# Order of the loads behind a first batch of attention, small copies on another engine, and a reduction held back

## The chip, the cores and the metric

One core of one Trainium2 chip. The metric is the device time of one execution in microseconds (us). Each kernel is executed several times; a number such as "842.15 median" is over its runs in the fast state, and all runs compared here are of that state. The profile is one execution, and its span is 1.7 to 1.9 us shorter than the time of the same execution.

Engines are named as in the profile: PE is TensorE (matmuls), DVE is VectorE, ACT is ScalarE, POOL is GpSimd, SP is the engine that issues the DMA transfers here.

## The reference

Four batches of block-sparse attention (8 heads, 768 positions, head dimension 64): each query sees the keys within 16 positions and, for each block of 32 keys, the maximum of the keys and the mean of the values. The result, 768 x 512 per batch, goes through a Fourier mix, a normalization and a two-layer MLP.

```python
k_sum = k.reshape(B, H, nb, block, D).max(axis=3)
v_sum = v.reshape(B, H, nb, block, D).mean(axis=3)
scores_l = scale * np.matmul(q, k.transpose(0, 1, 3, 2))      # masked to |i - j| < 16
scores_s = scale * np.einsum('bhsd,bhnd->bhsn', q, k_sum) + np.log(block)
# softmax over both, times [v, v_sum]; heads side by side -> x (B, 768, 512)
X = np.fft.fft(np.fft.fft(x, axis=1), axis=2)
u = x + np.real(X)
un = (u - mean(u)) / np.sqrt(var(u) + 1e-06)
out = u + np.maximum(un @ w_ch1, 0.0) @ w_ch2                 # 512 -> 2048 -> 512
```

## The kernel before

The change sits in the first 60 us. The first batch's attention goes by pairs of heads, g = 0 to 3. For each pair, `prepare` transposes keys and queries on PE, copies them out of PSUM on ACT (`kt`, `qt`) and takes the block maxima of the keys on DVE (`km`). `wide_scores` gives the probabilities `p`, and `wide_values` multiplies them by the values (`vw`, loaded by `load_values`, in rows of 256 bytes). The result x is "folded" on DVE (sums and differences of mirrored columns), and the folded tiles are the input of the first Fourier matmuls, `y`; then come the mix matmuls `mx`, the normalization, transposes `unt`, and the hidden layer `hx`. Beside this runs the second batch's attention. `load(b, g)` loads keys and queries of a pair, `load_raw(n)` loads packed weights ("words") up to the n-th, `block_sums` loads and adds the values of a block, `near` is a mask table.

```python
def first_attention():
    ...
    for g in range(NP - 1):
        p[g + 1] = wide_scores(0, g + 1, ...)
        wide_values(0, g, p[g], x)
        load_values(*following(0, g, 2))          # g = 1: the last pair's values
        for par in range(2):
            fold_sequence(par, g)
        if g == 0:
            get_tables(0)                         # fs, fs, fd
        if g < NP - 2:
            prepare(0, g + 2)
            load(1, g)                            # next batch's keys and queries
            sum_values(0, g + 1)
        if g == 0:
            load_raw(2)                           # weight words
            fetch(out=near, ...)
        ...
    fold_halves(0, 0)
    wide_values(0, NP - 1, p[NP - 1], x)
    for par in range(2):
        ...
        fold_ends(0, par, ...)
```

```python
# prepare(b, g), after the transposes
    for s in range(2):
        nc.scalar.copy(out=dst[...], in_=ps[D * s:D * (s + 1)])    # kt, then qt
nc.vector.tensor_reduce(out=km[:, 0:nb], in_=kt[...], op=ALU.max, axis=AX.X)

# fold_ends(b, par, zw, fg): three small copies among the DVE folds
nc.scalar.copy(out=fg[:, :, 0:DM:HD], in_=zw[:, :, 0:DM:HD])              # 128 x 6
tt(fg[:, :, 1:Q], ..., ADD)
nc.scalar.copy(out=zqs[b][:, par], in_=zw[:, :, Q])                       # 128 x 3
...
nc.scalar.copy(out=fg[:, :, DM - 1:DM], in_=zw[:, :, HD + Q:HD + Q + 1])  # 128 x 3

# the main part
with tc.manual_schedule(engines={PE, DVE}):       # order as written; elsewhere a scheduler orders
    first_attention()
load_raw(4)
...
block_sums(1, 0)
def second_attention():
    prepare(1, 0)
    ...
drive((gen_fourier(0), 4, 600), (first(weights, 66), 12, 0), (first(attn, 6), 1, 0))
```

## Time and profile before

| | before |
|---|---|
| time, median of 4 | 842.15 us (842.01 to 842.78) |
| span of the profiled run, mean clock | 839.8 us, 0.989 |
| PE busy | 808.4 us, 96% |
| longest PE wait | 8.8 us, for the last pair's values |
| first y, first mx, first unt, first hx | 59.26, 71.97, 88.68, 95.73 us |
| first o, first ox (second layer), end | 150.51, 237.06, 839.8 us |

The last two rows are landmarks: the start of the first matmul of each stage. Where the kernel runs the same matmuls afterwards, a change can be followed as the shift of each landmark, and the difference between two neighbouring shifts says in which stage time was won or lost.

How PE reaches the first Fourier matmul is seen in its timeline (start, us, engine, line, operation, output<-inputs, sizes, count):

```profile
58.55 0.77 PE L756 MATMUL sc<-qt,kt 64*64 64x32 f32 x36
59.26 2.56 PE L1070 MATMUL y<-fs,fold 128*128 128x193 f32 x8
```

Scores of the next batch (sc) stand ahead of y in PE's order and fill its time while the folds are made, so y follows them without a gap.

### The profile page before, as it was taken

Reading aid. Unit: us, or ns where it says so; the run is one execution under the profiler, and the core shown is the slowest. Engines: PE = TensorE matmul, PEld = TensorE weight load, DVE = VectorE, ACT = ScalarE, POOL = GpSimd, SP = SyncE. Lnnn points to the kernel's source line nnn. Section 1 sums busy time; section 2 is a strip of 40 time slices with the busy share of each in tenths; the row PEclk is TensorE's granted clock in tenths of the full one; section 3 lists DMA queues with packets and bytes.
Section 4 is the critical chain, followed back from the end, with each engine's and each line's share of the span. In section 5 each row is a group of like instructions: output and inputs, shape, how many; then the busy total and the mean of one; then the engine's idle time right before and its main releaser. Section 6 shows DMA issues by size and latency. Waiting matters only on the chain.

```text
span 839.8 us, 14695 instructions
## 1 busy us (share of the span) xinstructions
PE 808.4 (96%) x6074; PEld 578.8 (69%) x6074; DVE 487.7 (58%) x1117; ACT 255.2 (30%) x567; POOL 12.8 (2%) x21
## 2 busy tenths in 40 slices
PE   8959899999999999999999999999999999999997
PEld 5748655545578855786668875788667875786586
DVE  4758989986996743543357822552347842532352
ACT  3523847542635123113233404120322502101100
POOL 0000000000000200011000000000000000000000
PEclk9969999999999999999999999999999999999999
DMA  9995799959633276255552244413412225205001
GB/s 227 244 230 86 165 282 245 298 198 321 212 116 124 76 271 170 87 114 193 132 120 89 78 171 171 126 26 103 158 46 81 77 82 232 88 0 219 1 26 54
DMA packets 101612, 120.55 MB, mean 144 GB/s; under 512 B 50560, under 2 KB 83552, under 8 KB 101344
## 3 DMA queue, kind: packets, MB, share of 16 engines
q1 hardware_dynamic: 100848, 119.31, 48.7%
q8 instruction: 50, 0.82, 0.4%
q10 hardware_dynamic: 688, 0.20, 0.1%
q14 instruction: 26, 0.21, 0.1%
HBM read 96.96 MB, written 22.54 MB: 142 GB/s over the span
## 4 chain that ended last, share of the span: by engine, by line
PE 83%; DVE 6%; DMA 4%; ACT 4%; SPq 1%; issue 1%; ACTq 0%; DVEq 0%
PE hx L1171 18%; PE ox L1235 17%; PE hz L1171 9%; PE oz L1235 9%; PE y L1070 4%; PE hy L1171 4%; PE oy L1235 4%; PE o L1212 3%; PE mx L1027 2%; PE sc L756 2%; DMA vb<-in_v_dram 2%; ACT qt L696 1%; ACT kt L696 1%; PE y L1074 1%; PE unt L1149 1%; PE av L789 1%
## 5 line engine op out<-in xcount | busy, mean ns | idle before, releaser
L1171 PE MATMUL hx<-u,w 128*128 128x384 f32 x512 | 187.2, 492 | 6.9 <-DVE h L562 2.8
L1171 PEld LDWEIGHTS hx<-u,w 128*128 128x128 f32 x512 | 94.5, 190 | 72.2 <-DVE h L562 6.4
L1171 PE MATMUL hz<-u,w 128*128 128x384 f32 x256 | 93.5, 487 | 0.1
L1235 PE MATMUL ox<-w,s 128*128 128x256 f32 x336 | 81.5, 381 | 0.3
L1235 PE MATMUL oz<-w,s 128*128 128x256 f32 x336 | 80.7, 379 | 0.0
L1235 PE MATMUL ox<-w,h 128*128 128x256 f32 x336 | 78.4, 381 | 0.0
L1171 PEld LDWEIGHTS hz<-u,w 128*128 128x128 f32 x256 | 48.4, 190 | 34.5 <-ACT h L1188 1.3
L562 DVE TENSOR_TENSOR x<-ox,x 128x256 f32<-128x256 f32 x84 | 35.4, 422 | 62.1 <-PE ox L1235 62.0
L1235 PEld LDWEIGHTS ox<-w,h 128*128 128x128 f32 x336 | 63.3, 190 | 10.7 <-DVE x L562 1.1
L1235 PEld LDWEIGHTS oz<-w,s 128*128 128x128 f32 x336 | 63.5, 190 | 8.3
L1235 PEld LDWEIGHTS ox<-w,s 128*128 128x128 f32 x336 | 62.5, 190 | 9.2 <-DVE x L562 1.1
L562 DVE TENSOR_TENSOR h<-hx,h 128x384 f32<-128x384 f32 x32 | 17.8, 555 | 65.8 <-PE hx L1171 65.8
L1181 ACT COPY h<-hx 128x384 f32<-128x384 f32 x32 | 15.3, 477 | 129.1 <-PE hx L1171 117.4
L562 DVE TENSOR_TENSOR h<-hy,h 128x384 f32<-128x384 f32 x32 | 17.8, 556 | 59.2 <-PE hy L1171 56.0
L1171 PE MATMUL hy<-u,w 128*128 128x384 f32 x128 | 48.2, 499 | 0.0
L1212 PE MATMUL o<-w,h 128*128 128x512 f32 x96 | 42.8, 597 | 0.0
L1235 PE MATMUL oy<-w,h 128*128 128x256 f32 x168 | 39.9, 379 | 0.0
L1197 ACT ACTIVATE h<-hx 128x384 f32<-128x384 f32 x32 | 15.6, 488 | 79.4 <-PE hx L1171 79.4
L1070 PE MATMUL y<-fs,fold 128*128 128x193 f32 x192 | 37.5, 342 | 0.2
L1171 PEld LDWEIGHTS hy<-u,w 128*128 128x128 f32 x128 | 24.7, 194 | 17.6 <-DVE w L562 0.8
L1070 PEld LDWEIGHTS y<-fs,fold 128*128 128x128 f32 x192 | 31.7, 193 | 6.3 <-issue 4.9
L1235 PEld LDWEIGHTS oy<-w,h 128*128 128x128 f32 x168 | 31.9, 190 | 4.3
(138 smaller groups left out, 1075.6 us busy)
## 6 DMA issues: line engine op xcount, KB each, us to landing
w<-dw SPq DMA_DIRECT2D x44, 896.0 KB, 5.6
words<-in_moe_w_ch_dram SPq DMA_DIRECT2D x32, 512.0 KB, 6.7
dw<-w SPq DMA_DIRECT2D x12, 896.0 KB, 7.0
vw<-in_v_dram SPq DMA_DIRECT2D x47, 192.0 KB, 5.7
kn<-in_k_dram SPq DMA_DIRECT2D x16, 384.0 KB, 4.5
qn<-in_q_dram SPq DMA_DIRECT2D x16, 384.0 KB, 5.4
out_dram<-x SPq DMA_DIRECT2D x24, 256.0 KB, 2.0
fs<-c_fs SPq DMA_DIRECT2D x8, 579.0 KB, 3.5
```

The source lines that it names most:

```text
L562: nc.vector.tensor_tensor(out=out, in0=in0, in1=in1, op=op)
L696: nc.scalar.copy(out=dst[D * e:D * (e + 1), s:S:2], in_=ps[D * s:D * (s + 1)])
L756: nc.tensor.matmul(ps[h][r:r + 64, i, :], kt[rows, o:o + 64], qt[rows, o:o + BLOCK], start=True, stop=True)
L789: nc.tensor.matmul(av[r][32 * j:32 * (j + 1), t, :], p[rows, h, i - NB2 * h, :], vw[rows, i, :], start=(t == 0), stop=False, skip_group_ch ...
L1027: nc.tensor.matmul(out, y[:, g], table, start=True, stop=last, skip_group_check=True)
L1070: nc.tensor.matmul(y, fgs[par][:, st, P * g:P * (g + 1)], fs[par][:, g % 2, st, :], start=(st == 0), stop=(st == HT - 1))
L1074: nc.tensor.matmul(ps[0:1, par:par + F2 + 1], zq[:, par, s2:s2 + 1], fs[par][:, 0, s2, :], start=False, stop=False, skip_group_check=True)
L1171: nc.tensor.matmul(ps, w[:, a, kk, :], u[:, r, kk, :], start=start and kk == 0, stop=stop and kk == 1, skip_group_check=True)
L1181: nc.scalar.copy(out=c11, in_=X)
L1197: nc.scalar.activation(out=c21, in_=X, func=AF.Relu)
L1212: nc.tensor.matmul(ps, h[:, n, hf, P * t:P * (t + 1)], wt[2, b, j][:, 2 * hf:2 * hf + 2, :], start=(n, hf) == (0, 0), stop=(n, hf) == (NC ...
L1235: nc.tensor.matmul(ps, left[a][:, n, :], wt[2, b, j][:, r, :], start=start and n == 0, stop=stop and n == NC - 1, skip_group_check=True)
```

## The change

Its intent: the last pair's values are needed at 41.6 us, but next batch's keys and queries, weight words and `near` are issued ahead of them. The change puts them behind. It takes six small copies off ACT, and ties the next batch's key maxima on DVE behind the folds, so that a late `kt` cannot hold the folds.

```diff
@@ prepare
-        nc.vector.tensor_reduce(out=km[:, 0:nb], in_=kt[...], op=ALU.max, axis=AX.X)
+        with tc.issue_after(marks["fold", 0]) if (b, g) == (1, 0) else ExitStack():
+            nc.vector.tensor_reduce(out=km[:, 0:nb], in_=kt[...], op=ALU.max, axis=AX.X)
@@ first_attention
                 prepare(0, g + 2)
-                load(1, g)
                 sum_values(0, g + 1)
-            if g == 0:
+            if g == NP - 3:
+                load_raw(1)
+                load(1, 0)
                 load_raw(2)
-                fetch(out=near, in_=dr["near"].ap()...)
-            if g == NP - 3:
                 sum_values(0, g + 2)
@@ fold_ends
-        nc.scalar.copy(...)                       # three of them
+        copy = nc.scalar.copy if b else nc.gpsimd.tensor_copy
+        copy(...)                                 # three of them
@@ main part
         first_attention()
+    fetch(out=near, in_=dr["near"].ap()...)
     load_raw(4)
+    load(1, 1)
```

The numbers of most later lines rise by one to four: L740 is L741 in the changed kernel, L1070 is L1072, L1171 is L1173.

More of the change, by code (lines that the diff above doesn't have):

```diff
@@ L696, in prepare @@
                         nc.scalar.copy(out=dst[D * e:D * (e + 1), s:S:2], in_=ps[D * s:D * (s + 1)])
-        nc.vector.tensor_reduce(out=km[:, 0:nb], in_=kt[:, W:W + S].rearrange("p (n f) -> p n f", f=BLOCK),
-                                op=ALU.max, axis=AX.X)
+        with tc.issue_after(marks["fold", 0]) if (b, g) == (1, 0) else ExitStack():
+            nc.vector.tensor_reduce(out=km[:, 0:nb], in_=kt[:, W:W + S].rearrange("p (n f) -> p n f", f=BLOCK),
+                                    op=ALU.max, axis=AX.X)
         nat[b, g] = qt
@@ L828, in first_attention @@
                 prepare(0, g + 2)
-                load(1, g)
                 sum_values(0, g + 1)
-            if g == 0:
+            if g == NP - 3:
+                load_raw(1)
+                load(1, 0)
                 load_raw(2)
-                fetch(out=near, in_=dr["near"].ap().rearrange("p (h i) c -> p h i c", h=2))
-            if g == NP - 3:
                 sum_values(0, g + 2)
@@ L863, in fold_ends @@
             zqs[b] = spool.tile([P, 2, HT], FP, tag="zq", bufs=2, name=f"zq_{b}")
-        nc.scalar.copy(out=fg[:, :, 0:DM:HD], in_=zw[:, :, 0:DM:HD])
+        copy = nc.scalar.copy if b else nc.gpsimd.tensor_copy
+        copy(out=fg[:, :, 0:DM:HD], in_=zw[:, :, 0:DM:HD])
         tt(fg[:, :, 1:Q], zw[:, :, 1:Q], zw[:, :, HD - 1:Q:-1], ADD)
-        nc.scalar.copy(out=zqs[b][:, par], in_=zw[:, :, Q])
+        copy(out=zqs[b][:, par], in_=zw[:, :, Q])
         nc.vector.memset(fg[:, :, Q:Q + 1], 0.0)
         tt(fg[:, :, Q + 1:HD], zw[:, :, 1:Q], zw[:, :, HD - 1:Q:-1], SUB)
-        nc.scalar.copy(out=fg[:, :, DM - 1:DM], in_=zw[:, :, HD + Q:HD + Q + 1])
+        copy(out=fg[:, :, DM - 1:DM], in_=zw[:, :, HD + Q:HD + Q + 1])
         tt(fg[:, :, HD + 1:HD + Q], zw[:, :, HD + 1:HD + Q], zw[:, :, DM - 1:HD + Q:-1], SUB)
@@ L1321, in _main_program @@
         first_attention()
+    fetch(out=near, in_=dr["near"].ap().rearrange("p (h i) c -> p h i c", h=2))
     load_raw(4)
+    load(1, 1)
     nc.vector.memset(vs, 0.0)
```

## The prediction

> **What bounds the kernel now.** I read the page first. TensorE (PE) is busy 96% of an 839.8 us span and holds 83% of the chain that ended last, so nearly all of the kernel is matmul time that this change does not touch. What can move is idle PE time, so I read PE's waits next, longest first:
>
> ```profile
> PE av L740 <- DMA vw<-in_v_dram: 8.8, 1, 8.8
> PE hx L1171 <- DVE h L562: 2.8, 2, 1.5
> PE hx L1171 <- ACT h L1181: 2.4, 3, 1.1
> PE sc L717 <- DVE km L697: 1.8, 2, 1.2
> ```
>
> Columns: total us, times, longest. One wait stands out: the value matmuls of the first batch's last pair of heads wait once, 8.8 us, for their values (vw) to come from memory. Everything else is under 3 us. The chain in order of time shows where that wait comes from (start, us, what):
>
> ```profile
> 39.95 1.64 PE av L740 x48
> 41.60 1.60 SPq L549
> 43.25 7.01 DMA vw<-in_v_dram
> 50.26 0.14 issue
> 50.40 3.07 PE av L740 x47
> 53.47 0.85 PE qk L694 x3
> ```
>
> Pair 2's values product runs at 39.95 and takes 1.64 us; pair 3's would follow at 41.6 and starts at 50.40. It then takes 3.07 us for the same 48 matmuls, so there is a second cost besides the wait. The timeline of the DMA-issuing engine says why the values are late:
>
> ```profile
> 33.42 0.38 SPq L549 DMA_DIRECT2D kn<-in_k_dram  x1
> 33.90 0.62 SPq L549 DMA_DIRECT2D qn<-in_q_dram  x1
> 34.61 4.92 SPq L549 DMA_DIRECT2D words<-in_moe_w_ch_dram  x2
> 39.58 1.28 SPq L549 DMA_DIRECT2D near<-c_near  x1
> 40.96 7.61 SPq L549 DMA_DIRECT2D vw<-in_v_dram  x6
> ```
>
> Next batch's keys and queries, two pieces of weight words and the table near are issued ahead of vw, though none is needed before 53 us. The table by stretches shows the two costs together (us; then busy time of PE, PEld, DVE, ACT, POOL; granted clock, DMA share, GB/s):
>
> ```profile
> 34.00:38.00 4.00, 3.10 (x40) 2.08 (x38) 3.92 (x5) 2.46 (x5) 0.00 (x0) 1.00 0.98 356
> 38.00:42.00 4.00, 3.55 (x74) 2.72 (x74) 2.73 (x7) 1.16 (x3) 0.14 (x1) 1.00 1.10 326
> 42.00:46.00 4.00, 0.00 (x0) 0.00 (x0) 2.98 (x7) 0.20 (x1) 0.00 (x0) 1.00 1.16 307
> 46.00:50.00 4.00, 0.00 (x0) 0.00 (x0) 0.00 (x0) 0.00 (x0) 0.00 (x0) 0.50 0.89 107
> 50.00:56.00 6.00, 5.60 (x60) 5.20 (x60) 1.97 (x5) 1.55 (x4) 0.14 (x1) 0.50 1.22 224
> 60.00:64.00 4.00, 4.00 (x15) 2.44 (x15) 4.00 (x11) 0.95 (x4) 0.00 (x0) 0.61 1.08 271
> ```
>
> PE does nothing from 41.6 to 50.4 while the DMA engines are full, and the clock falls to half at 46, because PE was idle, and again from about 59.7 to 63.1.
>
> **What the Trainium skill says.** "TensorE: Matmul & The Clock Gate", part 1 (the HAM clock gate): the clock is halved after an idle window and restored after a busy one, windows of 3413 ns that run freely. The trace agrees: in half-microsecond slices the clock changes at about 46.0, 56.3, 59.7 and 63.1, which are multiples of 3.41 us apart. "DMA: Bandwidth & Descriptors", section Queues, rings and completion order: each DMA engine consumes one issuer's descriptors in ring order. The trace agrees in the order of landing (issue plus time to landing: kn 41.4, qn 42.8, words 44.3 and about 46.3, near 48.3, vw 49.3 to 50.9). Same page, Why small descriptors are slow: 256-byte descriptors lose bandwidth; here the vw rows (256 bytes) move at about 130 to 160 GB/s against 326 to 356 GB/s for the longer ones. "GPSIMD Engine Reference", section 4.1: one-input elementwise work there is roughly at line rate. In the trace two 128x24 copies on GpSimd take 0.37 us together, and ScalarE takes 0.19 to 0.20 us for each of the small fold copies, so the move should cost nothing.
>
> **The change part by part.**
>
> Values earlier. The order of instructions in the built kernel puts the six vw transfers directly behind the Fourier tables (fs, fs, fd), so issue can start at 33.4 in place of 40.96. They need pair 1's product to be done, which it is at 31.3. In front of them in the ring no longer stand kn, qn (384 KB each), two words (512 KB each) and near (384 KB): 2176 KB, 2.23 MB. At 326 to 356 GB/s that is 6.3 to 6.8 us, so vw lands at 50.3 - 6.5 = about 43.7. A check from the other side: fd lands at 39.6, vw is 560 KB at 0.15 MB/us, 3.8 us, giving 43.4. The values product then runs from 43.8 to 45.5, at full clock (1.67 us, as for pair 2). The wait becomes about 2.2 us, not zero.
>
> Keys and queries later. Before, kn had landed at 41.4 and cost nothing. Now kn, qn and the first words go behind vw. The issuing queue itself blocks when much is outstanding (one 20 KB vw issue took 3.92 us), so I put the first words' issue at about 41.5, kn at 42.5 and qn at 43. With 3.4 and 4.4 us to landing, as those two took at 48.7 and 49.1 with little ahead of them, plus 1 to 1.5 us for the words ahead, kn lands at about 47 and qn at 48.5. This is a new wait of PE, 1.5 us after the values product. From the first key transposes to the first score matmul the chain before takes 57.52 - 53.40 = 4.1 us: transposes, four kt copies (2.04 us) and two of the four qt copies (1.0 us) on ScalarE. At full clock some 0.3 us less. In the new PE order one score matmul stands before the Fourier matmuls y, so y starts at about 47 + 3.9 = 50.9 in place of 59.26: 8.4 us earlier.
>
> Key maxima behind the folds. In the trace before, the reduction km (0.95 us) sits in VectorE's order ahead of the folds and waits 1.1 us for kt. Behind the folds it lets them start when x is ready: values end 45.5, four x pieces and the subtraction 2.0 us, two folds 1.0, first end fold 0.5, so y's input is there at about 49.2, before kt and qt. With the reduction in its old place the folds would end at about 52 and hold y by 1 us. So this part is worth about 1 us, already contained in the 50.9.
>
> Small copies. Six ScalarE copies of 0.19 us go, 1.1 us off an engine with a 30% share. They free y from waiting behind the kt and qt copies in ScalarE's order. GpSimd has nothing else to do. Worth 0 to 0.5 us, also contained.
>
> What is given back. Before y, the kernel before had already done 40 score matmuls and two ss products (0.30 + 0.83 + 0.77 = 1.9 us in the timeline); now all but one come after the mix matmuls, so 1.6 to 1.8 us of PE work goes behind. And the clock: between 45.5 and 50.9 PE has only some 1 us of work, so a 3.41 us window will nearly surely be idle enough and y begins at half clock until a full window has passed, costing half of 3.4 to 6.8 us less what passed before; I take 2.5 us. The kernel before loses half of 3.4 us, 1.7, there. Extra loss 0.8.
>
> Sum: 8.4 - 1.7 - 0.8 = 5.9 us. After that PE is dense, but between 80 and 140 us it has 5.3 us of idle time that VectorE, ScalarE and the block-sum loads cause (the chain goes there through a vb transfer of 7.17 us at 114). VectorE moves forward by 8 us, more than PE, and the first weight store no longer stands ahead of those loads in the issue order, so I give 0.6 us back: a gain of 6.5 us. From 842.2 that is 835.7.
>
> **The rivals.**
> Keys as the new wait in full: if kn and qn come only at 50, with the value rows of the next batch mixed in, y starts at 54 and the gain is 5.2 - 1.7 = 3.5 minus the clock, 839 or so. For it: the issuer blocks when the ring is full. Against: in the order built, kn and qn precede the next 64-row values.
> The full 8.8 us and its clock loss go: if keys land by 45.5, y starts at 49.4, and if the clock windows fall well, the gain is 9 to 10 us, 832 to 833. For it: DMA is free for 1 us before the tables arrive. Against: 2.2 us of values wait cannot go.
> Gain lost downstream: if the weight conversion on VectorE (9.3 to 10 of every 10 us busy from 80 to 110) were bound by the words' arrival, later words would hold the first hidden layer. First words land at about 45 and 48, and are converted from 64.4 before and about 55 after, so I give this little. A changed scheduling order until 240 us can give or take 1 us in any direction.
>
> **Range and chances.** The clock (1 us either way), kn's landing (1.5) and the order downstream (1.5) add to some 2.5 us: 832.5 to 839.0. A gain of 2% would need 16.8 us, twice the whole wait with its clock loss; a loss of 2% has nothing in the diff to make it. Chances 0.01, 0.98, 0.01.
>
> **What would show it.** The values wait should be 1.5 to 3 us, and their 48 matmuls take 1.7 us. A new wait of the first L694 transposes for kn should show, 1 to 2 us. The first y should start at 50 to 52, behind one score matmul, partly at half clock. DVE's folds should have no km before them, and GpSimd six copies of 0.1 to 0.3 us. If y starts after 53 the keys are mis-sized; if y starts near 51 and the end moves by less than 4 us, the loss is downstream, between 60 and 240 us. A clock that stays full through 45 to 55 would make it faster than I say.

## The result, and the profile after

The changed kernel takes 836.18 us (median of 4, 835.32 to 838.18) against 842.15. The ratio is 0.9931, 95% interval 0.991 to 0.9952. Here and below a ratio is the mean time of one kernel's fast runs over the mean of the other's fast runs in the same rounds, so it is not quite the ratio of the medians. The profiled spans are 833.5 and 839.8 us, 6.3 apart. Both range and class of the prediction held; the sum, 6.5 us, was right to 0.5 us in the median. Its terms were less right.

The DMA-issuing engine in the changed kernel (start, us, output<-input, count):

```profile
33.62 7.89 SPq L549 DMA_DIRECT2D vw<-in_v_dram  x6
41.60 0.39 SPq L549 DMA_DIRECT2D words<-in_moe_w_ch_dram  x1
42.05 0.50 SPq L549 DMA_DIRECT2D kn<-in_k_dram  x1
42.59 0.54 SPq L549 DMA_DIRECT2D qn<-in_q_dram  x1
43.18 1.49 SPq L549 DMA_DIRECT2D words<-in_moe_w_ch_dram  x1
```

The values are issued at 33.62, not 40.96; the queue then takes 7.89 us for six issues, so words, keys and queries are issued only from 41.6. PE's waits in the changed kernel between 30 and 100 us (total us, times, longest):

```profile
PE qk L694 <- DMA kn<-in_k_dram: 3.0, 1, 3.0
PE vs L780 <- DVE norm L1126: 1.8, 1, 1.8
PE qk L694 <- DVE fold L562: 1.4, 1, 1.4
PE av L741 <- DVE rec L745: 0.9, 1, 0.9
```

The 8.8 us for vw are gone. In this run the values product waits 0.9 us, and for a buffer, not for data. Two waits are new: PE waits 3.0 us for the next keys, and 1.4 us before the query transposes, which start at 49.74. The profile names a fold as their releaser, but the queries land at 49.6 (issued at 42.59, 7.0 us to landing), so either came last. PE's timeline:

```profile
42.65 1.80 PE L741 MATMUL av<-vw,p 128*64 128x65 f32 x48 [0.90 <-DVE rec L745]
47.47 0.85 PE L694 MATMUL qk<-ident,kn 128*128 128x128 f32 x6 [3.02 <-DMA kn<-in_k_dram]
49.74 1.51 PE L694 MATMUL qk<-ident,qn 128*128 128x128 f32 x6 [1.42 <-DVE fold L562]
51.77 0.42 PE L757 MATMUL sc<-qt,kt 64*64 64x32 f32 x2 [0.52 <-ACT qt L696]
52.12 2.94 PE L1072 MATMUL y<-fs,fold 128*128 128x193 f32 x8
```

The first y comes at 52.12, 7.1 us earlier than before, behind two score matmuls that wait for a copy of qt. The key transposes take 0.85 us and the query transposes 1.51 us for the same six matmuls, which is the clock. The table by stretches (us; then busy time of PE, PEld, DVE, ACT, POOL; granted clock, DMA share, GB/s):

```profile
42.00:46.00 4.00, 1.80 (x48) 1.69 (x48) 3.89 (x10) 0.00 (x0) 0.32 (x3) 1.00 0.80 231
46.00:50.00 4.00, 1.11 (x8) 0.93 (x9) 3.90 (x10) 1.91 (x4) 0.90 (x2) 0.90 1.20 289
50.00:56.00 6.00, 5.48 (x20) 4.00 (x19) 5.73 (x15) 2.67 (x7) 2.26 (x3) 0.50 1.10 194
```

Between 42 and 50 PE works 2.9 of 8 us, against 0 before; the clock falls at 49.2 and is back at 56.0, two windows of 3.41 us. Of the small copies, now on POOL, two rows of the timeline:

```profile
45.32 0.20 POOL L866 COPY fold<-fold 128x6 f32<-128x6 f32 x1 [3.27 <-DVE fold L562]
51.70 1.33 POOL L866 COPY fold<-fold 128x6 f32<-128x6 f32 x1 [2.90 <-DVE fold L562]
```

The same copy takes 0.20 us once and 1.33 us the other time. The Trainium skill, "GPSIMD Engine Reference", section 8 (Key points), says that the engine shares its SBUF interfaces with VectorE and contends with VectorE instructions that have two SBUF inputs. The trace fits: at 51.70 folds run on DVE, which read two inputs from SBUF; at 45.32 it is a product (x) that reads one of its two inputs from PSUM. All eleven profiles with these copies on POOL agree: the first copy takes 0.19 to 0.20 us, with DVE idle or at the reciprocal or product that read PSUM, and the second takes 1.33 us, always under folds. No run changes this overlap alone.

The shift of each landmark, from the two profiles (subtraction of start times):

| stage | before | after | shift | won in the stage |
|---|---|---|---|---|
| first y | 59.26 | 52.12 | 7.14 | 7.14 |
| first mx | 71.97 | 65.05 | 6.92 | -0.22 |
| first unt | 88.68 | 82.80 | 5.88 | -1.04 |
| first hx | 95.73 | 90.72 | 5.01 | -0.87 |
| first o | 150.51 | 145.18 | 5.33 | 0.32 |
| first ox | 237.06 | 230.69 | 6.37 | 1.04 |
| end | 839.8 | 833.5 | 6.3 | -0.07 |

Between mx and hx 1.91 us are given back. The second wait in the list above is part of it: PE's matmuls for the block sums (`vs`) of the next batch wait for DVE, which adds the loaded values late, among the steps of the normalization (DVE's timeline, changed kernel):

```profile
79.98 1.01 DVE L623 TENSOR_REDUCE vbs<-vb 96x64 f32<-96x512 f32 x1
80.98 0.17 DVE L1126 TENSOR_SCALAR norm<-norm 128x3 int32<-128x3 int32 x1
```

PE needs vbs from 79.3 and starts at 81.14. The window with this gap (79.9 to 83.3) has PE busy for 48% of it, and the clock is at half from 83.3 to 86.7. A half-clock window costs half its length, 1.7 us, when PE is busy in it; PE's idle time from mx to hx grew from 2.03 to 2.53 us; and the next batch's scores between the mix matmuls and the key transposes take 2.30 us in place of 1.72, since fewer of them were done before y. Together 2.8 us, more than the 1.91, so how the loss divides among the three is not settled.

### The profile page after: what moved, and what is told of

It is laid out like the page before. It is cut to its first block, busy times and chain, and to the rows that moved or that the text cites. A ratio compares the mean times of both kernels' runs of the same rounds, so it can differ in the third digit from the quotient of the medians.

```text
span 833.5 us, 14698 instructions
## 1 busy us (share of the span) xinstructions
PE 803.7 (96%) x6074; PEld 577.3 (69%) x6074; DVE 487.5 (58%) x1117; ACT 254.9 (31%) x561; POOL 16.1 (2%) x27
## 4 chain that ended last, share of the span: by engine, by line
PE 83%; DVE 10%; ACT 3%; issue 1%; DMA 1%; ACTq 0%; DVEq 0%
PE hx L1173 18%; PE ox L1237 17%; PE hz L1173 9%; PE oz L1237 8%; PE y L1072 4%; PE o L1214 4%; PE hy L1173 4%; PE oy L1237 4%; PE mx L1029 2%; PE sc L757 2%; DVE x L562 1%; PE unt L1151 1%; PE y L1076 1%; ACT qt L696 1%; PE av L790 1%
## 5 line engine op out<-in xcount | busy, mean ns | idle before, releaser
L1173 PE MATMUL hx<-u,w 128*128 128x384 f32 x512 | 186.2, 491 | 7.2 <-DVE h L562 3.3
L1173 PEld LDWEIGHTS hx<-u,w 128*128 128x128 f32 x512 | 94.5, 190 | 72.1 <-DVE h L562 7.0
L1173 PE MATMUL hz<-u,w 128*128 128x384 f32 x256 | 93.3, 487 | 0.0
L1237 PE MATMUL oz<-w,s 128*128 128x256 f32 x336 | 80.7, 379 | 0.0
L1173 PEld LDWEIGHTS hz<-u,w 128*128 128x128 f32 x256 | 48.4, 190 | 34.3 <-ACT h L1190 1.1
L1173 PE MATMUL hy<-u,w 128*128 128x384 f32 x128 | 46.6, 487 | 0.0
L1072 PE MATMUL y<-fs,fold 128*128 128x193 f32 x192 | 37.9, 344 | 0.1
L1072 PEld LDWEIGHTS y<-fs,fold 128*128 128x128 f32 x192 | 32.1, 195 | 6.3 <-issue 4.9
L1173 PEld LDWEIGHTS hy<-u,w 128*128 128x128 f32 x128 | 24.2, 190 | 17.1 <-DVE w L562 0.6
```

The costliest lines, as they stand in the source:

```text
L1072: nc.tensor.matmul(y, fgs[par][:, st, P * g:P * (g + 1)], fs[par][:, g % 2, st, :], start=(st == 0), stop=(st == HT - 1))
L1173: nc.tensor.matmul(ps, w[:, a, kk, :], u[:, r, kk, :], start=start and kk == 0, stop=stop and kk == 1, skip_group_check=True)
L1237: nc.tensor.matmul(ps, left[a][:, n, :], wt[2, b, j][:, r, :], start=start and n == 0, stop=stop and n == NC - 1, skip_group_check=True)
```

## The experiments

Twelve kernels in three visits to the chip, five rounds each, all correct. Each visit has its own runs of the kernel before (medians 842.54, 842.43, 843.07; 11 runs each). Times scattered more than on the first visit (836.72 against 836.18 for the same instructions), so effects of about 1 us are read from traces.

| kernel | median us | range of 6 runs | ratio to before | 95% interval |
|---|---|---|---|---|
| e0_same_stream | 836.72 | 834.43 to 840.34 | 0.9935 | 0.9911 to 0.996 |
| e1_loads_only | 838.32 | 833.91 to 839.16 | 0.9936 | 0.9909 to 0.9962 |
| e4_no_loads | 842.51 | 840.71 to 844.57 | 0.9999 | 0.998 to 1.0018 |
| e5_keys_first | 835.75 | 834.45 to 839.46 | 0.9926 | 0.9903 to 0.995 |
| e6_cold | 838.12 | 835.46 to 841.79 | 0.9941 | 0.9913 to 0.9969 |
| e6_warm | 836.64 | 835.5 to 841.62 | 0.994 | 0.9912 to 0.9968 |
| e2_km_ahead | 838.30 | 837.01 to 841.83 | 0.9947 | 0.9922 to 0.9972 |
| e7_sums_early | 835.13 | 832.45 to 840.17 | 0.9913 | 0.9881 to 0.9944 |
| e9_y_first | 834.68 | 833.23 to 837.39 | 0.9902 | 0.9874 to 0.9931 |
| e9_y_sums | 834.52 | 828.34 to 837.95 | 0.9883 | 0.9842 to 0.9923 |
| e9_sums_warm | 837.33 | 830.33 to 839.64 | 0.9909 | 0.987 to 0.9948 |
| e9_acts_sums | 834.27 | 829.84 to 834.97 | 0.9879 | 0.9849 to 0.9909 |

**Theory.** The whole gain is the load order; what limits it is the arrival of next keys and queries, the clock, and block sums that come later. **Rivals.** The copies or the tie carry part of the gain; or the folds on DVE, not the keys, set the start of y.

**1. The tie taken out.** The changed kernel without its third part:

```diff
-        with tc.issue_after(marks["fold", 0]) if (b, g) == (1, 0) else ExitStack():
-            nc.vector.tensor_reduce(...)
+        nc.vector.tensor_reduce(...)
```

> The changed kernel with its third part undone in the source: the key maxima are no longer tied to the folds. The built instruction streams of all five engines are the same, row by row, as those of the changed kernel, so once the loads are moved the third part should change nothing. My theory: 0.993 of the time before, as the changed kernel (its interval was 0.991 to 0.995), and the reduction still behind the folds. It is also the repeat that says how far two runs of one stream differ. Rival (the tie is worth about 1 us, as I predicted): 0.9942 or more.

In the build its instruction streams are those of the changed kernel, row by row on all five engines (the two traces show the same order too), so it is also a measure of the scatter. Ratio 0.9935 against 0.9931. In its profile the last pair's values product waits 2.2 us, the kn wait is 1.7 us and y starts at 53.29: the same program spreads by more than 1 us in each of these. What follows: with the loads moved, the scheduler puts the reduction behind the folds by itself, and the third part does nothing.

**2. The load order alone.** Tie and POOL copies undone:

```diff
-        copy = nc.scalar.copy if b else nc.gpsimd.tensor_copy
+        copy = nc.scalar.copy
```

> The load order alone; small copies on ScalarE, maxima untied. My theory (the load order makes the gain): the values wait is gone, the wait for kn is about 3 us, first y at 52 to 53, ratio 0.992 to 0.995. Rival (moving the copies to GpSimd carries part of it, because the y matmuls would wait behind the key and query copies on ScalarE): first y or the second group of y at least 1 us later than in the changed kernel, ratio 0.995 to 0.997.

The ratio is 0.9936, the whole effect. The trace holds a surprise: y starts earlier than in the changed kernel (PE's timeline).

```profile
49.66 2.78 PE L1071 MATMUL y<-fs,fold 128*128 128x193 f32 x8
```

49.66 against 52.12. In the build, PE's order differs: with the copies on ACT, y stands directly behind the query transposes; with the copies on POOL, the scheduler puts two score matmuls ahead of it, and those wait for qt. So the second part of the change costs time at this place. In this profile the head start is lost again, by a stall for which the profile names no releaser (PE's waits)

```profile
PE av L789 <- issue: 3.4, 1, 3.4
```

and by half-clock stretches at 80.0 to 83.4 and 86.8 to 93.7. Two of its six runs are near 834 us, four at 838 to 839. What that stall is stays open, but the DMA records hold a candidate: a 16 KB packet of an instruction queue (q8) starts inside it, at 84.67, and is done at 85.89; PE starts again at 87.21. The fourteen profiles have seven stalls without a releaser of more than 0.5 us, in five kernels, and in each PE starts 1.3 to 2.0 us after such a packet is done. So PE may wait for its own instructions there; no run tests it.

**3. Copies and tie without the load order.** The old order of loads in the changed kernel:

```diff
                 prepare(0, g + 2)
+                load(1, g)
                 sum_values(0, g + 1)
+            if g == 0:
+                load_raw(2)
+                fetch(out=near, ...)
             if g == NP - 3:
-                load_raw(1)
-                load(1, 0)
-                load_raw(2)
```

with `near` and `load(1, 1)` gone from the main part again.

> The opposite: the old load order with the copies on GpSimd and the maxima tied behind the folds. My theory: the 8.8 us values wait is all there, PE starts the values product at about 50.4, ratio 0.998 to 1.001 (the 2 us that the maxima held the folds are hidden behind the key and query copies, which hold the first y). Rival (the small parts matter by themselves): ratio 0.997 or less, first y before 58.

842.51 us, ratio 0.9999; the vw wait is 8.3 us and y starts at 58.88 (59.26 before). Copies and tie by themselves, under the old load order, are worth nothing that these runs can show (interval 0.998 to 1.0018).

**4. Keys ahead of the first words.**

```diff
             if g == NP - 3:
-                load_raw(1)
                 load(1, 0)
                 load_raw(2)
```

> The changed kernel with next batch's keys and queries ahead of the first weight words instead of behind. My theory (the new wait is keys and queries in the DMA queue, 512 KB of words ahead of them, about 1.5 us): kn lands at about 46 and qn at 47.5 to 48.5, the wait for kn shrinks from 3.0 to about 1.6 us and y starts at 50.5 to 51, ratio to before 0.991 to 0.992. Rival (the query transposes wait for VectorE's folds until 49.7, as the profile of the changed kernel names it): the query transposes still start at 49.7, y still at 52, ratio 0.993.

From issue to landing kn took 4.0 us in place of 5.3, and qn 4.8 in place of 7.0: the 512 KB of words ahead of them had cost 1.3 and 2.2 us. (One profile each; the same instructions as the changed kernel took 4.9 and 7.2 us in run 1.) The wait for kn vanished, but this profile can't be read as a clean test: a half-clock stretch at 12 to 19 us made PE 4.4 us late at the last score matmuls already (the value products start at 44.49, not 40.08), so the keys had time. First y at 53.55, only 9.1 us behind those products against 12.0 in the changed kernel. Ratio 0.9926: not told apart from the changed kernel.

**5. The clock.** A control in which `prepare(1, 0)` is placed by hand at the end of `first_attention`, without the tie, and the same with five dummy matmuls whose results are unused:

```diff
+            if (b, g) == (1, 0):                  # ahead of the k and the q transposes
+                ps = bank([P, 512], ...)
+                for _ in range(N):                # control: 0, 0, 0; warm: 3, 1, 1
+                    nc.tensor.matmul(ps, ident, rhs, start=True, stop=True)
```

Each is 128 x 512 (three stand ahead of the k transposes, one ahead of and one behind the q transposes); in the trace each is two matmul records.

> Control for the next two: the changed kernel with the second batch's first preparation placed by hand at the end of the first attention stage, so that the order of TensorE and VectorE there is fixed; the order of y is the same, the reduction comes directly behind the last fold. My theory: as the changed kernel, ratio 0.992 to 0.995, y first at 52, half clock over 4 to 7 us around 49 to 56. Rival: none, it is a control; if it differs by more than 1.5 us from the changed kernel, the next two are compared with it alone.

> The control with five idle-time matmuls of 128x512 (identity times a table, results unused) in the waits of TensorE: three before the key transposes, one before and one after the query transposes, 0.86 us each. My theory (the clock falls because TensorE idles there, and costs y half of about 3.9 us): no half clock between 44 and 60, y at full clock, the y stage about 2 us shorter, ratio to the control 0.9975 to 0.9985. Rival 1 (y is fed by the folds, so a faster clock only waits): y stage not shorter, new waits of y for folds. Rival 2 (the filling matmuls delay the transposes by more than they save): y starts 1 us or more later.

The stretch 50 to 54 us, the control first, then the warm kernel:

```profile
50.00:54.00 4.00, 3.48 (x14) 3.02 (x13) 4.00 (x10) 2.18 (x5) 2.26 (x3) 0.50 1.26 156
```

```profile
50.00:54.00 4.00, 4.00 (x22) 2.64 (x21) 4.00 (x11) 2.92 (x7) 2.21 (x3) 1.00 1.17 149
```

The control ran at half clock from 47.5 to 57.7, the warm kernel not at all between 42 and 80. From first y to first mx the warm kernel took 11.13 us in place of 13.77. It was 4.0 us ahead at mx and 2.3 at hx, but at the first o it was level (147.03, and 146.75 for the control): its hidden layer waited 3.2 us for DVE where the control's waited 2.3, and its clock fell at 80.7 and again at 128.5 (the control's at 112.3). The ratios to the kernel before are 0.994 (warm) and 0.9941 (control), so the 0.9975 to 0.9985 expected between the two was missed. The clock loss is real and of the size seen, but here a gain of the first 60 us is not a gain of the kernel. That this is so because VectorE has the same work left is likely, not shown. (In the warm kernel y also stands ahead of the scores, as in run 2, so the 1.3 us at first y are not the clock alone.)

**6. The reduction forced ahead of the folds.** `prepare(1, 0)` by hand between the two halves of the folds, without the tie:

```diff
             fold_sequence(par, NP - 1)
+            if par == 0:
+                prepare(1, 0)
```

> The changed kernel with the key maxima forced by hand into their old place, ahead of the folds of the first half. My prediction's reading: VectorE waits for the key copies until about 50.1, the folds end 2 to 3 us later and y starts at 53 to 54 instead of 52.1; ratio to the control 1.001 to 1.002. Rival (the folds have slack because the query copies hold y anyway until 51.8): y at 52.1 to 52.5, ratio 1.000.

DVE's timeline in this kernel:

```profile
50.55 0.95 DVE L697 TENSOR_REDUCE km<-kt 128x24 f32<-128x768 f32 x1 [3.14 <-ACT kt L696]
51.42 1.02 DVE L562 TENSOR_TENSOR fold<-wide 128x384 f32<-128x384 f32 x2
```

DVE stands for 3.14 us until kt is there, and only then folds. The first half of the folds is done at 54.3 (50.2 in the changed kernel). So the danger that the tie is meant for is real and costs some 4 us at the folds, but it has to be built by hand. That the late folds hold y is not shown: with this placement the scores also stand ahead of y in PE's order, and y follows them without a wait (PE's timeline).

```profile
54.64 1.28 PE L756 MATMUL sc<-qt,kt 64*64 64x32 f32 x36
55.85 2.62 PE L1073 MATMUL y<-fs,fold 128*128 128x193 f32 x7
```

The start of y at 55.85 lies behind the 53 to 54 expected, and the ratio, 0.9947, is not told apart from the control's 0.9941.

**7. Block sums loaded earlier.**

```diff
         first_attention()
+    block_sums(1, 0)
     fetch(out=near, ...)
     load_raw(4)
     load(1, 1)
 ...
-    block_sums(1, 0)
```

> The changed kernel with the second batch's block-sum values loaded ahead of near, the next words and the next keys. My theory (part of what was won at y is given back at 79 to 81, where the values product of the second batch waits 1.8 us for block sums that come late and were put among the norm steps): the block sums are added before the mix products come, the 1.8 us wait goes, the first hidden matmul starts 1 to 2 us earlier than 90.7, ratio 0.991 to 0.992. Rival (VectorE is the bound there in any order): the wait moves to the hidden layer, ratio 0.993.

The sums are ready some 12 us earlier (DVE's timeline):

```profile
68.13 1.04 DVE L623 TENSOR_REDUCE vbs<-vb 96x64 f32<-96x512 f32 x1
```

DVE does them at 64.8 to 69.2, where it was idle for part of the time. The wait of vs is gone, the clock stays full from 55.3 to beyond 100, and hx starts at 89.13 (90.72), 37.1 us after y in place of 38.6. The profiled span is 833.8, so some of it is lost later. Ratio 0.9913, not told apart from the changed kernel's. The edit moves both the load and the place of the adds in DVE's order; which of the two does it isn't told apart.

**8. y ahead of the scores, and combinations.** The scores of the next batch's first pair tied behind the first y:

```diff
+                    if (b, par, g, st) == (0, 0, 0, HT - 1):
+                        marks["y", 0] = ins.ins              # the y matmul
 ...
+                    with tc.issue_after(marks["y", 0]) if (b, g) == (1, 0) else ExitStack():
                         nc.tensor.matmul(ps[h]..., kt..., qt...)
```

> The changed kernel, with the first score matmuls of the second batch tied behind the first y matmuls, nothing else. Theory (in the changed kernel two score matmuls, which wait for the qt copies until 51.8, stand ahead of y in PE's order because the small copies left ScalarE): y starts at about 50.2, when the last fold piece is done, not at 52.1; its length to the first mx is 11.0 us plus half of the half-clock time that falls in it, so mx starts at 63 to 64.5 (65.05 in the changed kernel); the median comes 1 to 2 us below that of the changed kernel, 834 to 835.5. Rival (the folds hold y in any case): y stays at 51.8 or later and the median within 0.5 us of 836.2.

y starts at 50.54 (about 50.2 expected) and the median is 834.68, within the 834 to 835.5 expected; mx at 61.85 is earlier than the 63 to 64.5 expected. PE's timeline:

```profile
50.54 1.81 PE L1073 MATMUL y<-fs,fold 128*128 128x193 f32 x8
```

The rival that the folds hold y falls: they were done at 50.3, and the two score matmuls were what held it. Of the 3.2 us at mx, 1.6 us are luck with the clock: half clock ended at 51.2, so 0.67 us of it fell into the y stage and not 3.88.

The tie, and the block sums early as in 7:

> The same tie, and block sums of the second batch loaded ahead of near and the next words. Theory (two independent losses, they add): y at about 50.2, no wait of vs for the norm steps, hx at about 87 (90.7 in the changed kernel), median 832.5 to 834.5. Rival (what is won before 80 us is taken back by VectorE, which has the same work left): hx at 89 or later, median no lower than that of the tie alone.

Ratio 0.9883, median 834.52; the gain over the tie alone is inside the intervals. This profile had a half-clock stretch at 11 to 18 us, so PE came to the last value products 3.1 us late, and all landmarks must be read with that. The vs wait is 0.2 us, and hx started at 88.81, 36.8 us after y. One of PE's waits is worth a look:

```profile
PE y L1073 <- POOL fold L872: 1.2, 1, 1.2
```

This reads as if the slow copies on POOL held y. They hardly do: the last of them is done at 51.89, but the fold on DVE that the first y also reads is done at 51.84. PE and the folds were late together. The expected hx near 87 and the independence of the two gains were not shown by this profile.

Block sums early and the dummy matmuls (the edits of 7 and 5):

> Block sums early, and the dummy matmuls that keep the clock up until y. Theory (the half-clock windows cost about 1.7 us each): no half clock between 45 and 75, y at about 50.7, mx at about 61.8, no vs wait and so no idle window at 78 to 81, hx at about 86.5, median 832 to 834. Rival (PE gets ahead of VectorE and waits there instead): mx at 61.8 but hx at 88 or later, with waits of PE for DVE or ACT between 62 and 88 that sum to 2 us more than in the changed kernel, median 834 or more.

A miss. The values came late in this profile (3.3 us wait, product at 44.84) and the clock fell at 44.8, before the dummies could act. mx came at 64.71. The median, 837.33, is above that of the same block sums without dummies.

Block sums early, and the copies back on ACT (the edits of 7 and 2): of the change only the load order is left.

> Block sums early, and the small fold copies on ScalarE as before the change; PE's order is then that of the tied kernel. Theory (where the copies run matters only through PE's order): y at about 49.7 to 50.2, mx and hx within 0.7 us of the tied kernel with block sums early, medians equal within 1 us. Rival (copies on ScalarE hold y or the qt copies): y at 51 or later, or PE waits for qt.

y at 50.08, mx at 61.73, hx at 85.46, 35.4 us after y. Median 834.27, ratio 0.9879 (0.9849 to 0.9909), and all six runs at or below 834.97, where of ten runs of the changed kernel's instructions one was (834.43). It beats the kernel before clearly and the changed kernel probably; the two were not run in the same visit. The landmarks of e9_y_sums lie too far off to compare within 0.7 us, for the late start of that profile; the medians agree within 0.3 us.

A lead at a landmark is not yet a gain. In this profile the lead on the changed kernel is 5.3 us at hx and 4.2 us at the first ox, but 0.1 us at 320 us: PE waits 2.1 us for DVE before a later hx (1.0 us in the changed kernel), a half-clock window follows from 297.2 to 300.6, and the spans end up at 833.2 and 833.5 us. With y first (e9_y_first) 3.7 us at hx become 0.5 us at the end. These are single profiles, and the changed kernel's is of the fastest of its four runs, but the early leads are larger than what the medians gain.

**What the clock adds up to.** Over all fourteen profiles the time from first y to first mx, less half of the half-clock time that falls in it, is one number:

| kernel | y to mx | half clock in it | y to mx less half of it |
|---|---|---|---|
| before | 12.71 | 3.41 | 11.01 |
| changed | 12.93 | 3.88 | 10.99 |
| e0_same_stream | 13.39 | 4.89 | 10.94 |
| e1_loads_only | 12.43 | 3.04 | 10.91 |
| e5_keys_first | 12.63 | 3.29 | 10.98 |
| e6_cold | 13.77 | 5.68 | 10.93 |
| e6_warm | 11.13 | 0 | 11.13 |
| e7_sums_early | 12.65 | 3.33 | 10.98 |
| e9_y_first | 11.31 | 0.67 | 10.97 |
| e9_y_sums | 12.86 | 3.78 | 10.97 |
| e9_sums_warm | 11.00 | 0 | 11.00 |
| e9_acts_sums | 11.65 | 1.35 | 10.97 |
| e2_km_ahead | 12.92 | 3.88 | 10.98 |
| e4_no_loads | 12.46 | 2.94 | 10.99 |

PE is busy without gaps there, so nothing but its clock moves this stage. Whole runs go with the clock too: over the 72 runs of the twelve kernels, taken about each kernel's own mean, time falls by 0.69 us for each 0.001 of mean granted clock (correlation -0.79). One window at half clock in an 838 us run lowers that mean by 3.41 x 0.5 / 838 = 0.002, by that slope 1.4 us. So much of the scatter of several us goes with how many such windows a run draws (0.79 squared, 62% of its variance); the waits that come before such windows are counted in it.

## Why the prediction was right, point by point

**The wait removed.** Right. It left 2.2 us for late values; the profiles of this load order in which PE was not late itself show 0.9 to 2.2 us (0.9 in the changed kernel, 2.2 in the same instructions again), and one 3.3. The values product takes 1.80 us for the 1.67 of the prediction.

**Keys and queries as the next wait.** The mechanism was right, a term was too small. kn landed at 47.3 (47 predicted), qn at 49.6 (48.5 predicted): "plus 1 to 1.5 us for the words ahead" was right for kn (1.3 in run 4) and too small for qn (2.2). From the key transposes to y it took 4.65 us, not 3.9. So y came at 52.12, not 50.9, and the term "8.4 us earlier" was 7.14. The PE wait for kn was 3.0 us, not 1 to 2, since the values were done earlier (44.45, not 45.5).

**Small copies.** This step failed: "Worth 0 to 0.5 us, also contained." On POOL they took up to 1.33 us, not 0.1 to 0.3: "the move should cost nothing" left out what runs on DVE beside them. Above all they changed PE's order: the prediction saw the score matmul ahead of y in the new order, and took it as given. Tying it behind moved y to 50.54 (run 8), with the copies on ACT y stood at 49.66 and 50.08; the last of these differs from run 7 (52.00) in the copies alone.

**The reduction.** "Worth about 1 us" was mis-sized, and not owed to the change. Where the reduction does stand ahead, it costs about 4 us at the folds (run 6; that y is held so long is not shown); but without the tie the built kernel is the same (run 1). The prediction compared with the order of the trace before, not with the order that the scheduler would make once the loads had moved. That could have been seen from a build alone.

**The clock.** The extra loss of 0.8 us was 0.24: half of 3.88 less half of 3.41 us, inside the y stage. The two half-clock windows were foreseen.

**What is given back behind y.** "1.6 to 1.8 us of PE work" was too large. Its 1.9 us adds durations that overlap (from 57.52 to 59.26 it is 1.74 us, at full clock), and two ss matmuls alone took 0.83 us there, where eight side by side take 0.85 us in the changed kernel. Done behind the mix, this work adds 0.58 us there (2.30 in place of 1.72). The 1.91 us lost between mx and hx hold more idle time and one half-clock window besides, behind a wait for block sums. The prediction did not see the load of these sums, now issued at 56.28, behind others, and their adds among the normalization's steps. It named losses between 60 and 240 us only as a chance, and with another cause.

**Downstream.** +0.6 was predicted, 1.29 us came (0.32 + 1.04 - 0.07). The cause given, VectorE running ahead, does not show between hx and o: the changed kernel waits 2.3 us for DVE before hx there, the kernel before 1.2, but the kernel before has a half-clock window (117.7 to 121.1, 1.7 us) that the changed one lacks. So the 0.32 at least is owed to the clock, by luck; the 1.04 was not traced. The rival of a late word conversion did not show.

So the sum held, 7.14 - 0.22 - 1.91 + 1.29 = 6.3 against 8.4 - 0.8 - 1.7 + 0.6 = 6.5, because the first term was 1.3 us too large, and the losses and the gain behind it were off by 0.6, 0.2 and 0.7 us, mostly the other way. The mechanism for values, keys and the clock was right; that the errors of the terms cancel is luck.

## What to carry to other kernels

Where a transfer that is needed soon stands in a queue behind transfers that are needed late, moving it gives most of its wait, and the next thing to come late in the queue takes the rest; follow each moved load to its consumer, also 40 us on. A scheduler answers a change of engines or loads with another order: compare the built order of each part of a change by itself before a gain is ascribed to it. Read gains of a few us from landmarks and the granted clock of single profiles, since windows at half clock scatter whole runs by as much; and follow a lead to the end of the profile before it is called a gain.

## What the Trainium skill lacked or had wrong

- "TensorE: Matmul & The Clock Gate" speaks of idle and busy windows without a share. Twelve profiles here (all but e2_km_ahead and e4_no_loads), cut into windows of 3.41 us by their own clock changes (154 us each): all 16 full-clock windows with PE busy up to 45% were followed by half clock; from 46 to 75% ten of 55 were; of the half-clock windows all 11 up to 89% busy stayed at half, and 26 of 28 from 91% on returned to full. The shares are the profile's, whose matmul ends are modelled.
- The same page says that the window runs freely and that the warm-up varies by run. These runs put a size to it for a long kernel: 0.69 us per 0.001 of mean clock, and 834.43 to 840.34 us for one set of instructions.
- "GPSIMD Engine Reference" has no figure for very small copies or for the contention that it names: copies of 128x6 and 128x3 took 0.19 to 1.33 us, and 0.19 to 0.20 us on ScalarE.
- "DMA: Bandwidth & Descriptors": nothing says how long an issuing engine can stand at one issue. Here six issues of value rows took 7.89 us, and in the kernel before one issue of a 20 KB transfer 3.92 us, and that, with the order in the ring, set when keys could be issued.
- No page has a time that PE loses to the fetch of its own instructions. The seven stalls without a releaser here, 0.5 to 3.4 us, all end 1.3 to 2.0 us after a 16 KB packet of an instruction queue is done; that they are such losses is not tested.
